# Spreading a unit's decay logarithms by one product, and adding the state sum earlier, in a chunked mLSTM with two expert layers behind it

## The chip, the cores and the metric

The kernel runs on one core of a Trainium2 chip. The metric is the device time of the whole program in microseconds. A core has a matrix engine (PE, with its weight loads shown apart as PEld), a vector engine (DVE), a scalar engine (ACT), a general engine (POOL), and a sync engine (SP) that here only issues DMAs. Each engine runs its own instructions strictly in the order in which they were issued to it. Whatever is needed from another engine is waited for by semaphores.

## The reference, cut to what matters

Three stages follow one another: a gated linear attention (mLSTM) with a running stabiliser, an expert layer in which tokens are assigned greedily under a capacity, and a dense layer with an ELU.

```python
for t in range(S):                         # B=4, H=8, S=768, D=40
    m_new  = np.maximum(f_gate[:, :, t] + m, i_gate[:, :, t])
    f_stab = np.exp(f_gate[:, :, t] + m - m_new)
    i_stab = np.exp(i_gate[:, :, t] - m_new)
    C = f_stab[..] * C + i_stab[..] * (v k^T)
    n = f_stab[..] * n + i_stab[..] * k
    y[:, :, t] = sigmoid(o) * (C q) / np.maximum(np.abs(n q), 1.0)
# x = y as (3072, 320)
logits = x @ w_gate                        # 8 experts, 384 tokens each, greedy by logit
out[mask] = np.maximum(x[mask] @ w1[e], 0.0) @ w2[e]
h = out @ w_in;  g = elu(h);  result = g @ w_out
```

## The kernel before

The attention is done in chunks of 64 tokens: twelve chunks, and for each chunk two units of 2 batches by 8 heads, so 24 units. Unit u is chunk u // 2. The two batches of a unit lie on partitions 0 to 63 and 64 to 127. `Attention.run` is a pipeline over units written out by hand: iteration u works on unit u and prepares u + 1 (called v) and u + 2 (called w). Nothing reorders it; the order of the calls is the order on each engine.

What the names are, by the lines of the profile:

- **Logarithms.** `maximum` (L233) scans the stabiliser m. `logs` (L242 to L248) makes the decay logarithm ac and the input logarithm gi on 32 rows (batch and head). `split` (L257 to L264) writes each as three bfloat16 parts, fp and pb, on 96 rows; each part is copied by ACT and subtracted by DVE (L260, L261).
- **Decay weights.** `decay(w)` (L310 to L316) builds in one bank pF the logarithm of the 64 x 64 decay matrix of all 8 heads: a mask (L310), eight products of 64 columns, one for each head, whose stationary operand `sel` picks the head's rows of fp (L312), and a product for the inputs' side (L314). ACT takes the exponential (W, L316). `decays` (L323 to L334) makes the decays Dt and De over whole chunks.
- **Scores and values.** `scores(w)` (L301) and `values(u)` (L376) are interleaved on PE. `weigh(v)` (L355) multiplies scores by W into P, which `values(v)` needs in the next iteration.
- **State.** `recall(v)` (L390) is q times the state C of the chunk before, and is interleaved with `state(u)` (L403), the unit's own contribution pC. `seed(v)` (L366) writes the decayed recall into the output bank pO, on which `values(v)` then accumulates. `fade(v)` (POOL: L343 kt, L345) prepares the decayed keys and the decayed old state. `add_state(u)` (L414; L416 in the first chunk) adds pC to it. That sum is what `recall` of unit u + 2 reads, in the next iteration.
- **Output.** `gates(u)` (L423 to L428 on DVE, L429 on POOL) makes x; `turn` (L445) transposes it in the next iteration, and `logits` (L459) follows.
- **Fill.** From iteration 2 on, pieces of the later stages' weights are converted between the attention's own steps by `fl(i)`. The weights arrive as 8 bytes for a number; a piece takes ACT cg (L918), ACT cF (L925), DVE cF (L931), DVE cF (L934), ACT wih (L999) and POOL wil (L1001), or similar lines. `early` (L656 to L676) sorts finished logits.

The order on DVE within iteration u, from L502 on, is weigh(v), gates(u), seed(v), then the fill pieces, and add_state(u) behind them. `logs` and `split` over the ten later chunks (640 columns) stand at the start and in iterations 0 to 2.

After the attention come the first routing round and then the two layers, whose order is set by a planner with fixed costs; there the instructions of each engine stay as they are.

Of the kernel before, what the change touches and what calls it, by code (L numbers as in the profile page):

```python
# [8 lines left out]
F32 = mybir.dt.float32  # L9
F32R = mybir.dt.float32r  # L10
BF = mybir.dt.bfloat16
# [108 lines left out]
class Attention:  # L120
# [4 lines left out]
    def __init__(self, nc, tc, consts, qk, vk, ig, fg, wg, xd, L, ident):  # L125
# [50 lines left out]
        V.tensor_tensor(pair, i3[:, :16], i3[:, 16:], op=ALU.add)  # L176
        self.sel = one.tile([96, 16, 2, 64], BF, name="sel")
        V.tensor_copy(self.sel, i3.rearrange("p (r m) -> p m r", r=2)[:, :, :, None].to_broadcast([96, 16, 2, 64]))
        self.one_m = one.tile([96, 16, 64], BF, name="one_m")
# [10 lines left out]
        self.wr = one.tile([96, 2, 64], BF, name="wr")  # L190
        A.activation(self.wr, self.half[:, :, None].to_broadcast([96, 2, 64]), AF.Copy)
        self.i3 = i3
        self.Dt = one.tile([128, NS, 16], F32, name="Dt")
# [42 lines left out]
    def logs(self, n0, n1):  # L236

        gi, gf, m, keep, ac = self.g
        V = self.nc.vector
        a, b = n0 * 64, n1 * 64  # L240
        t = slice(a, b)
        V.tensor_tensor(gf[:, t], gf[:, t], m[:, t], op=ALU.add)  # L242
        V.tensor_tensor(gf[:, t], gf[:, t], m[:, a + 1:b + 1], op=ALU.subtract)
        if n0 == 0:
            V.memset(gf[:, 0:1], 0.0)
        V.tensor_tensor_scan(ac[:, t], keep[:, t], gf[:, t], 0.0, op0=ALU.mult, op1=ALU.add)
        V.tensor_tensor(gi[:, t], gi[:, t], m[:, a + 1:b + 1], op=ALU.subtract)
        V.tensor_tensor(gi[:, t], gi[:, t], ac[:, t], op=ALU.subtract)  # L248

    def split(self, n0, n1):  # L250

        gi, gf, m, keep, ac = self.g
        A, V = self.nc.scalar, self.nc.vector
        t = slice(n0 * 64, n1 * 64)
        for k in range(3):
            p, q = self.fp[k * 32:k * 32 + 32, t], self.pb[k * 32:k * 32 + 32, t]
            A.activation(p, ac[:, t], AF.Copy)  # L257
            A.activation(q, gi[:, t], AF.Copy)
            if k < 2:
                V.tensor_tensor(ac[:, t], ac[:, t], p, op=ALU.subtract)  # L260
                V.tensor_tensor(gi[:, t], gi[:, t], q, op=ALU.subtract)  # L261
                yield
        for r in range(2):
            A.activation(self.fb[:, n0:n1, r], self.pb[:, t].rearrange("p (n t) -> p n t", t=64), AF.Copy,  # L264
                         scale=self.half[:, r:r + 1])

    def load_qk(self, u):
# [37 lines left out]
    def decay(self, u):  # L305
# [4 lines left out]
        PE.matmul(p, self.idb, self.low, start=True, stop=False)  # L310
        for h in range(8):
            PE.matmul(p[:, h], self.sel[:, bp * 8 + h].rearrange("p r t -> p (r t)"), self.fp[:, n * 64:n * 64 + 64],  # L312
                      start=False, stop=False)
        PE.matmul(p, self.fb[:, n].rearrange("p r t -> p (r t)"), self.one_m[:, bp * 8:bp * 8 + 8], start=False, stop=True)  # L314
        self.W[u] = self.two.tile([128, 8, 64], F32, name="W", bufs=3)
        A.activation(self.W[u], p, AF.Exp)  # L316

    def decays(self, n0, n1):

        A, PE = self.nc.scalar, self.nc.tensor  # L320
        k = n1 - n0
        x = self.two.tile([96, 16, 10], BF, name="fx", bufs=1)[:, :, :k]
        self.nc.vector.tensor_tensor(x, self.one_m[:, :, :k], self.fp[:, None, n0 * 64 + 63:n1 * 64:64].to_broadcast([96, 16, k]),  # L323
# [7 lines left out]
        e = p[:, 256:256 + k * 16]  # L331
        PE.matmul(e, self.wr.rearrange("p r t -> p (r t)"), x.rearrange("p m n -> p (m n)") if k == 10 else x[:, :, 0], start=True, stop=True)
        A.activation(self.De[:, :, n0:n1], e.rearrange("p (m n) -> p m n", n=k), AF.Exp)
# [141 lines left out]
    def run(self, hook, fill, pull):  # L475
        later = self.split(2, NS)
        self.zeros(0)
        for u in range(NU):
# [4 lines left out]
            self.both(self.values(u), self.scores(w))  # L483
            if u == 0:
                self.decays(1, 2)
            if u < 3:
                next(later, None)
            if v < NU:
# [1112 lines left out]
```

## Time and profile before

| | |
|---|---|
| three runs | 763.69, 769.18 and 766.97 us, median 766.97 |
| the profiled execution | 769.29 us, of it 767.5 us span |
| attention, 24 units | about 0 to 154 us |
| routing round and first gathers | about 154 to 194 us |
| the two layers | about 194 to 767 us |

The page gives each engine's busy time and 40 slices of the span. Busy shares are means over stages with different limits, so each stage is read by itself. In the layers PE is busy nearly all the time. In the attention no engine is, and the rows on waits and on single units say what ends each step.

### The profile page before, as it was taken

The page shows a single profiled execution, that of the slowest core. Times are in us where ns is not written, and L with a number is a line of the kernel's source. Part 1 is how long each engine was busy: PE and PEld are TensorE (multiplying, and loading weights), DVE is VectorE, ACT ScalarE, POOL GpSimd, SP SyncE. Part 2 cuts the span into 40 slices and gives each one's busy share as a digit, 9 for nine tenths or more (in the row PEclk, how much of TensorE's full clock was granted, in tenths as well). Part 3 has the DMA queues.
Part 4 walks back from the last instruction along what each step waited for, and adds up shares of the span by engine and source line. Part 5 has one row for each costly group of instructions (what it writes and reads, how often), then busy time and mean ns, then how long its engine had stood idle before and what let it go on. Part 6 is the DMA issues. An engine that isn't in the chain of part 4 may idle for free.

```text
span 767.5 us, 17906 instructions
## 1 busy us (share of the span) xinstructions
PE 702.1 (91%) x7228; PEld 640.0 (83%) x7232; DVE 536.9 (70%) x1610; ACT 377.3 (49%) x804; POOL 180.1 (23%) x242
## 2 busy tenths in 40 slices
PE   6787888834999999999999999999999999999994
PEld 4555666622989998999999999999999999999994
DVE  8674787677878878875796698669768834841551
ACT  5553544423555735751673376256527734742542
POOL 5473643226111310401221120112022220001001
PEclk9999999955999999999999999999999999999998
DMA  9686878125200500500220220022013321100000
GB/s 310 201 256 197 241 206 249 39 80 166 95 0 6 173 26 1 177 1 27 83 95 27 72 82 25 26 83 95 1 44 106 108 82 34 36 0 26 1 1 26
DMA packets 22435, 67.29 MB, mean 88 GB/s; under 512 B 3536, under 2 KB 7632, under 8 KB 22352
## 3 DMA queue, kind: packets, MB, share of 16 engines
q1 hardware_dynamic: 14240, 35.12, 15.2%
q0 software_dynamic: 8064, 30.94, 12.3%
q8 instruction: 56, 0.92, 0.5%
q14 instruction: 27, 0.22, 0.1%
q10 hardware_dynamic: 48, 0.10, 0.0%
HBM read 58.28 MB, written 7.86 MB: 86 GB/s over the span
## 4 chain that ended last, share of the span: by engine, by line
PE 69%; DVE 12%; issue 11%; ACT 4%; DMA 2%; POOL 1%; POOLq 0%; ACTq 0%; DVEq 0%
PE ph L1176 31%; PE acc L1315 6%; PE acc L1319 6%; PE acc L1316 6%; PE acc L1283 3%; PE acc L1285 2%; PE acc L1284 2%; PE pR L390 2%; PE pO L376 1%; PE acc L1270 1%; PE pX L445 1%; PE acc L1272 1%; PE ph L1129 1%; DVE C L414 1%; PE pr L773 1%
## 5 line engine op out<-in xcount | busy, mean ns | idle before, releaser
L1229 DVE SCALAR_TENSOR_TENSOR e<-e,ph 128x384 f32<-128x384 f32 x128 | 70.4, 550 | 51.6 <-ACT e L1226 50.9
L1225 ACT ACTIVATE e<-ph 128x384 f32<-128x384 f32 x128 | 62.3, 487 | 80.7 <-PE ph L1176 75.8
L1176 PE MATMUL ph<-yh,wih 128*128 128x384 f32 x256 | 89.5, 349 | 0.6 <-DVE xl L1137 0.3
L1193 ACT ACTIVATE gh<-ph 128x384 fp32r<-128x384 f32 x64 | 31.5, 491 | 115.1 <-PE ph L1176 90.4
L1176 PE MATMUL ph<-yh,wil 128*128 128x384 f32 x256 | 86.6, 338 | 0.0
L1325 POOL DMA_INDIRECT out_dram<-ot,idx x24 | 24.0, 998 | 218.8 <-ACT ot L1046 215.9
L1053 DVE TENSOR_TENSOR gl<-e,gh 128x384 fp32r<-128x384 f32 x128 | 71.0, 561 | 1.8 <-ACT gh L1046 0.3
L1226 ACT ACTIVATE e<-e 128x384 f32<-128x384 f32 x128 | 67.3, 526 | 4.0
L1315 PE MATMUL acc<-woh,gh 128*128 128x320 f32 x216 | 68.3, 316 | 0.0
L1200 DVE SCALAR_TENSOR_TENSOR gl<-ph,gh 128x384 fp32r<-128x384 f32 x64 | 35.2, 552 | 45.8 <-ACT gh L1193 45.7
L1319 PE MATMUL acc<-woh,gl 128*128 128x320 f32 x216 | 66.8, 309 | 0.4 <-DVE gl L1053 0.4
L1316 PE MATMUL acc<-wol,gh 128*128 128x320 f32 x216 | 66.7, 309 | 0.0
L1176 PE MATMUL ph<-yl,wih 128*128 128x384 f32 x256 | 66.5, 341 | 0.0
L1046 ACT ACTIVATE gh<-e 128x384 fp32r<-128x384 f32 x96 | 49.0, 514 | 11.4 <-DVE e L1229 11.1
L1319 PE MATMUL acc<-woa,gl 128*128 128x320 f32 x168 | 52.4, 312 | 0.8 <-DVE gl L1053 0.8
L1315 PE MATMUL acc<-woa,gh 128*128 128x320 f32 x168 | 53.1, 316 | 0.0
L1176 PEld LDWEIGHTS ph<-yh,wih 128*128 128x128 f32 x256 | 48.2, 188 | 4.7 <-ACT yh L1288 4.1
L1316 PE MATMUL acc<-wob,gh 128*128 128x320 f32 x168 | 51.9, 309 | 0.0
L1176 PEld LDWEIGHTS ph<-yh,wil 128*128 128x128 f32 x256 | 48.1, 188 | 0.0
L1176 PEld LDWEIGHTS ph<-yl,wih 128*128 128x128 f32 x256 | 46.2, 188 | 0.0
L1176 PE MATMUL ph<-xh,w1h 128*128 128x384 f32 x128 | 44.9, 351 | 0.0
L1176 PE MATMUL ph<-yh,wis 128*128 128x384 f32 x128 | 44.8, 350 | 0.0
(282 smaller groups left out, 1992.0 us busy)
## 6 DMA issues: line engine op xcount, KB each, us to landing
vk<-in_vk_dram SPq DMA_DIRECT2D x24, 484.0 KB, 5.6
qk<-in_qk_dram SPq DMA_DIRECT2D x20, 320.0 KB, 5.6
cx<-in_win_dram SPq DMA_DIRECT2D x8, 512.0 KB, 5.6
xd<-x SPq DMA_DIRECT2D x48, 80.0 KB, 3.8
wx<-in_wout_dram SPq DMA_DIRECT2D x9, 320.0 KB, 3.0
cx<-in_wout_dram SPq DMA_DIRECT2D x5, 448.0 KB, 5.2
qk<-in_qk_dram SPq DMA_DIRECT2D x4, 512.0 KB, 6.4
cx<-in_win_dram SPq DMA_DIRECT2D x4, 256.0 KB, 5.5
```

The costliest lines, as they stand in the source:

```text
L1046: self.nc.scalar.activation(out, x, AF.Copy)
L1053: self.nc.vector.tensor_tensor(out, x, y, op=ALU.subtract)
L1176: PE.matmul(p, w, x, start=k == 0, stop=k == 7)
L1193: nc.scalar.activation(h, p, AF.Relu)
L1200: nc.vector.scalar_tensor_tensor(l, p, 0.0, h, op0=ALU.max, op1=ALU.subtract)
L1225: nc.scalar.activation(e, p, AF.Relu, scale=-1.0)
L1226: nc.scalar.activation(e, e, AF.Exp, scale=-1.0)
L1229: nc.vector.scalar_tensor_tensor(e, e, -1.0, p, op0=ALU.add, op1=ALU.max)
L1315: PE.matmul(p, h[:, c], wh, start=f == 0, stop=False)
L1316: PE.matmul(p, h[:, c], wl, start=False, stop=False)
L1319: PE.matmul(p, l[:, c], wh, start=False, stop=f == 15)
L1325: s = nc.gpsimd.indirect_dma_start(out=self.out, out_offset=bass.IndirectOffsetOnAxis(ap=idx[:, t:t + 1], axis=0), in_=o, in_offset=None)
```

## The change

There are three parts. First, the eight products of 64 columns in `decay` become one of 512. For that `spread(n)` writes, once for a chunk, fe = heads x fp (96 rows, 512 columns, with each head's own rows only); chunk 0 on DVE, the other eleven on POOL, in odd iterations between fade(v) and gates(u). The stationary operand ws is one of two small constants. `sel` goes; `head`, `side`, `heads` and `ws` come. Second, the logarithms are made in three parts (chunks 0 to 1, 2 to 3 and 4 to 11) instead of two; the last part (512 columns) is computed in iterations 2 to 5. Third, `add_state(u)` moves from behind the fill pieces to right behind `seed(v)`.

```diff
-        self.sel = one.tile([96, 16, 2, 64], BF, name="sel")
-        V.tensor_copy(self.sel, i3.rearrange(...).to_broadcast([96, 16, 2, 64]))
+        V.tensor_tensor(head, pair[:, :8], pair[:, 8:], op=ALU.add)
+        V.tensor_reduce(side, pair.rearrange("p (b h) -> p b h", b=2), AX, ALU.max)
+        A.activation(self.head, head[:, :, None].to_broadcast([96, 8, 64]), AF.Copy)
...
+        for b in range(2):
+            A.activation(self.ws[b], self.wr, AF.Copy, scale=side[:, b:b + 1])
...
-        self.logs(0, 2)
-        for _ in self.split(0, 2):
+        for _ in self.decay_logs(0, 2):
             pass
+        self.spread(0, V)
...
         V.memset(self.pC, 0.0)
-        V.memset(self.pX, 0.0)
         self.decay(1)
         self.both(self.scores(1))
+        self.decays(1, 2)
         self.weigh(0)
+        V.memset(self.pX, 0.0)
         self.fade(0)
-        self.logs(2, NS)
+        self.spread(1, G)
+        for _ in self.logs(2, 4):
+            pass
...
-        for h in range(8):
-            PE.matmul(p[:, h], self.sel[:, bp * 8 + h]..., self.fp[:, n * 64:n * 64 + 64], ...)
+        PE.matmul(p, self.ws[bp].rearrange("p r t -> p (r t)"), self.fe[n], start=False, stop=False)
...
+    def spread(self, n, engine):
+        self.fe[n] = self.two.tile([96, 8, 64], BF, name="fe")
+        engine.tensor_tensor(self.fe[n], self.head, self.fp[:, None, n * 64:n * 64 + 64].to_broadcast([96, 8, 64]), op=ALU.mult)
...
     def run(self, hook, fill, pull):
-        later = self.split(2, NS)
+        later = {0: self.split(2, 4), 2: self.decay_logs(4, NS)}
+        when = [(0, 2), (0, 1), (2, 2), (2, 2), (2, 1), (2, 1)]
...
             if u == 2:
-                self.decays(2, NS)
+                self.decays(2, 4)
+            if u == 6:
+                self.decays(4, NS)
             if v < NU:
                 self.weigh(v)
+            if u < 6:
+                which, parts = when[u]
+                for _ in range(parts):
+                    next(later[which], None)
...
             if v < NU:
                 self.fade(v)
+            if u % 2 and u // 2 + 2 < NS:
+                self.spread(u // 2 + 2, self.nc.gpsimd)
             self.gates(u)
             if v < NU:
                 self.seed(v)
+            self.add_state(u)
             fl(1)
             fl(5)
             fl(2)
             if u > 0:
                 self.logits(u - 1)
-            self.add_state(u)
             fl(3)
```

The first place is DVE in iteration 7, from the seed of unit 8 to the seed of unit 9. C is the state sum, A a step of the early sorting, cF the conversion of a weight piece, P the weighed scores, rd and x the gates. Before:

```order
L366 TENSOR_TENSOR pO<-pR,Dt 128x8x41
L931 SCALAR_TENSOR_TENSOR cF<-cx,cF 128x512
L676 TENSOR_TENSOR A<-w_291,a_1147 128x32
L934 SCALAR_TENSOR_TENSOR cF<-cg,cF 128x512
L414 TENSOR_TENSOR C_170<-C_170,pC 128x8x41
L355 TENSOR_TENSOR P<-pS,W 128x512
L423 TENSOR_SCALAR rd<-pO 128x8
```

In the changed kernel, where the same lines are L388, L958, L703, L961, L436, L377 and L445:

```order
L388 TENSOR_TENSOR pO<-pR,Dt 128x8x41
L436 TENSOR_TENSOR C_178<-C_178,pC 128x8x41
L958 SCALAR_TENSOR_TENSOR cF<-cx,cF 128x512
L703 TENSOR_TENSOR A<-w_297,a_1126 128x32
L961 SCALAR_TENSOR_TENSOR cF<-cg,cF 128x512
L377 TENSOR_TENSOR P<-pS,W 128x512
L445 TENSOR_SCALAR rd<-pO 128x8
```

The state sum now stands ahead of the conversion; P still stands behind it.

The second place is DVE in iteration 3 of the changed kernel, from the state sum of unit 2 to the gates of unit 3. Before, the same stretch was:

```order
L414 TENSOR_TENSOR C_168<-C_168,pC 128x8x41
L355 TENSOR_TENSOR P<-pS,W 128x512
L423 TENSOR_SCALAR rd<-pO 128x8
L424 SCALAR_TENSOR_TENSOR rd<-pO,rd 128x8
L425 RECIPROCAL rd<-rd 128x8
L428 SCALAR_TENSOR_TENSOR x<-sg,pO 128x320
L366 TENSOR_TENSOR pO<-pR,Dt 128x8x41
```

Now:

```order
L436 TENSOR_TENSOR C_176<-C_176,pC 128x8x41
L958 SCALAR_TENSOR_TENSOR cF<-cx,cF 128x512
L961 SCALAR_TENSOR_TENSOR cF<-cg,cF 128x512
L377 TENSOR_TENSOR P<-pS,W 128x512
L260 TENSOR_TENSOR gi<-gi,m 32x512
L261 TENSOR_TENSOR gi<-gi,ac 32x512
L273 TENSOR_TENSOR ac<-ac,fp 32x512
L274 TENSOR_TENSOR gi<-gi,pb 32x512
L445 TENSOR_SCALAR rd<-pO 128x8
L446 SCALAR_TENSOR_TENSOR rd<-pO,rd 128x8
L447 RECIPROCAL rd<-rd 128x8
L450 SCALAR_TENSOR_TENSOR x<-sg,pO 128x320
```

Four logarithm steps of 512 columns now stand between P and the gates. In iteration 2 three others (L253, L254 and L258) stand at the same place, and in iteration 4 two.

The third place is POOL in iteration 7 (kt, the faded state and the gates' last product; wil belongs to the fill). Before:

```order
L343 TENSOR_TENSOR kt_178<-vk,W 128x8x40
L345 TENSOR_TENSOR C_168<-C_167,De 128x8x41
L429 TENSOR_TENSOR x<-x,rd 128x320
L1001 TENSOR_TENSOR wil<-cF,wih 128x512
L343 TENSOR_TENSOR kt_179<-vk,W 128x8x40
```

Now:

```order
L365 TENSOR_TENSOR kt_186<-vk,W 128x8x40
L367 TENSOR_TENSOR C_176<-C_175,De 128x8x41
L338 TENSOR_TENSOR fe<-heads,fp 96x512
L451 TENSOR_TENSOR x<-x,rd 128x320
L1028 TENSOR_TENSOR wil<-cF,wih 128x512
L365 TENSOR_TENSOR kt_187<-vk,W 128x8x40
```

The product fe stands ahead of the gates' product, in every second iteration.

## Rows read from the trace of the kernel before

**Rows 1.** The page, parts 1 and 2: PE's busy time; DMA share by slices.

```profile
PE 702.1 (91%) x7228; PEld 640.0 (83%) x7232; DVE 536.9 (70%) x1610; ACT 377.3 (49%) x804; POOL 180.1 (23%) x242
...
DMA  9686878125200500500220220022013321100000
```

**Rows 2.** Busy times by stretch: the attention without its start and end.

```profile
core 0: us, PE busy (x) PEld busy (x) DVE busy (x) ACT busy (x) POOL busy (x), PEclk, DMA share, GB/s
...
25.00:150.00 125.00, 101.68 (x3052) 74.77 (x3046) 86.14 (x219) 59.90 (x125) 58.97 (x68) 0.97 0.71 209
```

**Rows 3.** Waits, 25 to 150 us: us in total, times, longest.

```profile
DVE cF L931 <- ACT cF L925: 23.6, 10, 3.7
...
PE pR L390 <- DVE C L414: 12.1, 13, 2.1
...
PE pR L390 <- issue: 2.6, 2, 1.7
```

**Rows 4.** DVE in time, iterations 7 and 8: start, duration, what; idle before.

```profile
60.12 0.51 DVE L366 TENSOR_TENSOR pO<-pR,Dt 128x328 f32<-128x328 f32 x1 [1.47 <-PE pR L390]
63.51 0.69 DVE L931 SCALAR_TENSOR_TENSOR cF<-cx,cF 128x512 int32<-128x512 int32 x1 [2.89 <-ACT cF L925]
...
64.24 0.69 DVE L934 SCALAR_TENSOR_TENSOR cF<-cg,cF 128x512 int32<-128x512 int32 x1
64.85 0.49 DVE L414 TENSOR_TENSOR C<-C,pC 128x328 f32<-128x328 f32 x1
...
66.37 0.45 DVE L428 SCALAR_TENSOR_TENSOR x<-sg,pO 128x320 f32<-128x320 f32 x1
67.30 0.51 DVE L366 TENSOR_TENSOR pO<-pR,Dt 128x328 f32<-128x328 f32 x1 [0.48 <-PE pC L403]
```

**Rows 5.** PE, the first recall of unit 9.

```profile
65.39 0.27 PE L390 MATMUL pR<-C,qk 64*64 64x64 f32 x2 [1.76 <-DVE C L414]
```

**Rows 6.** DVE, the start of the program.

```profile
2.68 1.27 DVE L178 COPY sel<-i 96x2048 bf16<-96x2048 bf16 x1
...
5.80 0.28 DVE L248 TENSOR_TENSOR gi<-gi,ac 32x128 f32<-32x128 f32 x1
...
10.02 0.66 DVE L355 TENSOR_TENSOR P<-pS,W 128x512 f32<-128x512 f32 x1
10.61 0.80 DVE L242 TENSOR_TENSOR gf<-gf,m 32x640 f32<-32x640 f32 x1
...
14.52 1.24 DVE L248 TENSOR_TENSOR gi<-gi,ac 32x640 f32<-32x640 f32 x1
...
18.56 0.67 DVE L355 TENSOR_TENSOR P<-pS,W 128x512 f32<-128x512 f32 x1
...
22.78 0.67 DVE L355 TENSOR_TENSOR P<-pS,W 128x512 f32<-128x512 f32 x1
```

**Rows 7.** DVE, P of units 4 and 23.

```profile
34.84 0.68 DVE L355 TENSOR_TENSOR P<-pS,W 128x512 f32<-128x512 f32 x1
...
147.94 0.68 DVE L355 TENSOR_TENSOR P<-pS,W 128x512 f32<-128x512 f32 x1
```

**Rows 8.** PE, the last two of the three steps of one decay.

```profile
48.47 0.40 PE L312 MATMUL pF<-fp,sel 96*128 96x64 bf16 x8
48.70 0.38 PE L314 MATMUL pF<-one_m,fb 96*128 96x512 bf16 x1
```

**Rows 9.** A DVE and a POOL instruction at one time, from both engines' order of time.

```profile
82.38 1.19 DVE L666 TENSOR_TENSOR e<-e,w 128x32 f32<-128x32 f32 x1
...
82.23 1.29 POOL L1001 TENSOR_TENSOR wil<-cF,wih 128x512 fp32r<-128x512 f32 x1
```

**Rows 10.** Durations in ns, minimum, median and maximum, by line.

```profile
L429 POOL TENSOR_TENSOR x<-x,rd x24: 717/722/1200, 20.2 to 154.7; 128x320 f32<-128x320 f32 x24
...
L355 DVE TENSOR_TENSOR P<-pS,W x24: 661/681/692, 10.0 to 147.9; 128x512 f32<-128x512 f32 x24
...
L934 DVE SCALAR_TENSOR_TENSOR cF<-cg,cF x15: 607/681/1022, 33.8 to 143.2; 128x512 int32<-128x512 int32 x10, 128x448 int32<-128x448 int32 x5
```

More of the change, by code (lines that the diff above doesn't have):

```diff
@@ L176, in __init__ @@
         V.tensor_tensor(pair, i3[:, :16], i3[:, 16:], op=ALU.add)
-        self.sel = one.tile([96, 16, 2, 64], BF, name="sel")
-        V.tensor_copy(self.sel, i3.rearrange("p (r m) -> p m r", r=2)[:, :, :, None].to_broadcast([96, 16, 2, 64]))
+        head = one.tile([96, 8], BF, name="head")
+        V.tensor_tensor(head, pair[:, :8], pair[:, 8:], op=ALU.add)
+        side = one.tile([96, 2], F32, name="side")
+        V.tensor_reduce(side, pair.rearrange("p (b h) -> p b h", b=2), AX, ALU.max)
+        self.head = one.tile([96, 8, 64], BF, name="heads")
+        A.activation(self.head, head[:, :, None].to_broadcast([96, 8, 64]), AF.Copy)
         self.one_m = one.tile([96, 16, 64], BF, name="one_m")
@@ L191, in __init__ @@
         A.activation(self.wr, self.half[:, :, None].to_broadcast([96, 2, 64]), AF.Copy)
+        self.ws = [one.tile([96, 2, 64], BF, name=f"ws{b}") for b in range(2)]
+        for b in range(2):
+            A.activation(self.ws[b], self.wr, AF.Copy, scale=side[:, b:b + 1])
         self.i3 = i3
@@ L209, in __init__ @@
         self.maximum(0, 128)
-        self.logs(0, 2)
-        for _ in self.split(0, 2):
-            pass
+        for _ in self.decay_logs(0, 2):
+            pass
+        self.fe = {}
+        self.spread(0, V)
         self.opens(0)
@@ L245, in logs @@
             V.memset(gf[:, 0:1], 0.0)
+        yield
         V.tensor_tensor_scan(ac[:, t], keep[:, t], gf[:, t], 0.0, op0=ALU.mult, op1=ALU.add)
+        yield
         V.tensor_tensor(gi[:, t], gi[:, t], m[:, a + 1:b + 1], op=ALU.subtract)
@@ L265, in split, with decay_logs @@
                          scale=self.half[:, r:r + 1])
+    def decay_logs(self, n0, n1):
+        yield from self.logs(n0, n1)
+        yield
+        yield from self.split(n0, n1)
     def load_qk(self, u):
@@ L310, in decay @@
         PE.matmul(p, self.idb, self.low, start=True, stop=False)
-        for h in range(8):
-            PE.matmul(p[:, h], self.sel[:, bp * 8 + h].rearrange("p r t -> p (r t)"), self.fp[:, n * 64:n * 64 + 64],
-                      start=False, stop=False)
+        PE.matmul(p, self.ws[bp].rearrange("p r t -> p (r t)"), self.fe[n], start=False, stop=False)
         PE.matmul(p, self.fb[:, n].rearrange("p r t -> p (r t)"), self.one_m[:, bp * 8:bp * 8 + 8], start=False, stop=True)
@@ L321, in decays @@
         k = n1 - n0
-        x = self.two.tile([96, 16, 10], BF, name="fx", bufs=1)[:, :, :k]
+        x = self.two.tile([96, 16, k], BF, name=f"fx{k}", bufs=1)
         self.nc.vector.tensor_tensor(x, self.one_m[:, :, :k], self.fp[:, None, n0 * 64 + 63:n1 * 64:64].to_broadcast([96, 16, k]),
@@ L331, in decays @@
         e = p[:, 256:256 + k * 16]
-        PE.matmul(e, self.wr.rearrange("p r t -> p (r t)"), x.rearrange("p m n -> p (m n)") if k == 10 else x[:, :, 0], start=True, stop=True)
+        PE.matmul(e, self.wr.rearrange("p r t -> p (r t)"), x.rearrange("p m n -> p (m n)"), start=True, stop=True)
         A.activation(self.De[:, :, n0:n1], e.rearrange("p (m n) -> p m n", n=k), AF.Exp)
@@ L483, in run @@
             self.both(self.values(u), self.scores(w))
[L484 to L487, printed above, removed]
             if v < NU:
```

## The prediction

> **What bounds the kernel now.** I read the page first. PE is busy 91% of the span, but the slices of DMA show that loading is heavy in the first eight or so and light afterwards [rows 1]: the attention is one stage, the layers another. The change touches only the first 150 us, so the page's 91% says nothing about it. The busy times by stretch come next. From 25 to 150 us PE is busy 101.68 of 125 us, DVE 86.14, POOL 58.97 [rows 2]. No engine is full, so waits decide. The iterations from P of unit 4 (34.84) to P of unit 23 (147.94) take 113.1 us [rows 7], 5.95 us for each of 19.
>
> The view of waits tells which waits stand there. PE waits 12.1 us, 13 times, to begin `recall` until the state sum on DVE is done, and 2.6 us for nothing that the profile shows; DVE waits 23.6 us for the weight pieces from ACT [rows 3]. The unit view joins them. DVE finished the seed at 60.63, idled until ACT gave the piece at 63.51, did L931 and L934, and only then the state sum at 64.85 [rows 4]. PE stood 1.76 us and began the recall at 65.39 [rows 5]. The sum's own inputs were there long before: it stood idle behind a piece of weight conversion, by order alone.
>
> **The change part by part.**
>
> *The state sum moves up.* It follows the seed, so it could run at 60.6 instead of 64.85. What PE gains is the 1.76 us of [rows 5] here and 12.1 us in all [rows 3], if nothing else is late. What is late next: P still stands behind the piece. Without the sum in front of it (0.40 us from start to start [rows 4]), P begins 0.4 earlier, the gates end 0.4 earlier (66.4 in place of 66.82), and the next seed, which waited for PE until 67.30, may run at 66.4, 0.9 earlier and not 1.76. `values` needs that seed. So between a half and all of each wait comes back: in this unit PE's own work (transposes, decay, logits) still lies between recall and values, which covers the difference; where the early sorting or logarithms add DVE work, it does not. I take half of 12.1, 6.0 us, with ends 0 and 12.1.
>
> *The logarithms in three parts.* Before, DVE does five steps of 640 columns between the first and second P, from 10.61 to 15.7, and then waits for and does the first of the parts; the second P comes 8.5 us after the first and the third at 22.78 [rows 6]. Now five steps of 128 columns stand there, at 0.28 us each, about 1.5 us [rows 6]. `sel` goes (1.19 us from its start to the next step [rows 6]), but three more ACT copies and fe of chunk 0 on DVE, about 0.6 us by P's 0.66 on 512 columns [rows 6], come into the same chain; I count these as even. The second P then comes some 5 us earlier, and the third too. But the work is moved, not removed: the 512-column part is four fifths of the 640-column one. Of five steps that took 5.1 us, 4.1 remain, and four part subtractions come to 2.6, by four fifths of L242's 0.80 each [rows 6]. They now stand in iterations 2, 3 and 4 between P and the gates, on the way to the seed, which values waits for. In iteration 3 the part copies on ACT also stand behind W. DVE was idle there for a few microseconds, but ahead of the weight pieces, not ahead of the gates. So I let the 5 us of the start be given back by iteration 5, with 0.5 us left: -0.5, ends -4 and +1.5.
>
> *One product of 512 columns in place of eight of 64.* The eight start at 48.47 and the next step at 48.70: 0.23 us for all eight. The 512-column product behind them has 0.38 us against 0.40 for the group [rows 8]. The same columns at the same pace, so PE gains nothing; 24 x 0.0. Its weight loads lie under the product before. Fourteen instructions fewer per unit may move the unexplained PE stalls of [rows 3] by 2 us either way.
>
> *Spread on POOL.* Eleven products of 96 x 512 in bfloat16 with two inputs. No row has this form. From the 320-column product, 0.72 us [rows 10], and the 512-column one, 1.29 us [rows 9], I take 1.2; ends 0.7 and 1.3. POOL is busy less than half of the time [rows 2], and the product that needs fe comes an iteration later, so POOL's own time costs nothing. But the rows show a coupling: at 82.38 a DVE product of 32 columns took 1.19 us and ended with POOL's, which had run since 82.23 for 1.29 [rows 9]. L934, which reads two tiles of SBUF, takes 607 to 1022 ns; P, which reads one of its inputs from PSUM, 661 to 692, never more [rows 10]. So fe can hold the conversions and the logarithms, and not the seed, the sum, the gates or P themselves. Eleven times 1.2 is 13.2 us if each fe holds one such step on the path in full. Since it meets only these steps, I take a quarter, +3.3; ends 0 and 13.2.
>
> The rule to weigh here is the Trainium skill's, SBUF — State Buffer, section "SBUF: two separate sides": VectorE and GpSimd share one port pair, and whoever comes first holds it for its whole instruction while the other waits. Rows 9 and 10 agree with it. It speaks against this change, and what it would make of the time is the third rival.
>
> *Sum.* -6.0 - 0.5 + 0.0 + 3.3 = -3.2 us. The profiled execution took 769.29 us, so 766.1; it stands 2.3 above the median of the runs shown, 766.97. In terms of the median that is 763.8. The stages behind the attention begin when the last logits are there and keep their order, so what the attention gains is passed on whole: **764 us**.
>
> **Rivals.** All are given against the median.
>
> First, everything pays. All 12.1 us come back, the start keeps 1 us and fe meets nothing on the path: -13.1, **754 us**. For it: the units' PE work is shorter than 5.95 us without the waits (101.68 busy in 125 [rows 2] is 4.8 per iteration). Against: with PE at 4.8, the way through ACT's piece, L931, L934, P, gates and seed is hardly shorter.
>
> Second, nothing pays. DMA is busy six to nine tenths in the first eight slices [rows 1], and 0.71 in [rows 2]; an attention of shorter iterations needs its loads sooner and gets them at the same pace, or PE's unexplained stalls grow with them. The 6 us become waits on loads: **767 us**. For it: the slices with 9. Against: no wait of [rows 3] is on a load.
>
> Third, slower: the coupling of POOL and DVE. fe is ahead of the gates' product on POOL and meets the conversions. If two thirds of the eleven hold a step on the path, that is 8.8 us; conversions that are held also hold P, so of the 12.1 us only 3 come back. -3.0 - 0.5 + 8.8 = +5.3, **772 us**. It decides from the point at which three of the eleven are held in full, 3.6 us against 3.5. For it: [rows 9, 10]. Against: in a unit like that of [rows 4] the piece waits for ACT, not for POOL.
>
> That the one product does not do the work of eight is not a case that I can see; that it costs PE the same is part of the forecast.
>
> **How the numbers follow.** Forecast 0.50, everything pays 0.20, nothing pays 0.17, slower 0.13. A measurement of this kernel can tell about 1%, 7.7 us, from no change: under 759.3 is faster, over 774.6 slower. Faster: 0.16 from the first rival and 0.04 from the good end of the forecast, 0.20. Slower: a third of the third rival, 0.04, and 0.01 for what I have not seen, 0.05. Same 0.75. The forecast's own range is 759 to 768. The whole range takes in the better half of the first rival's times only from 755 on, and the third up to 770: low **755**, high **770**, with about 0.12 and 0.08 left out.
>
> **What would show it.** The wait of `recall` on the state sum should fall from 12.1 us to under 2. The wait of `values` on the seed should rise to several microseconds, above all in iterations 2 to 4, where P of unit 5 should come no earlier than one or two microseconds before its old time although the second P came some 5 earlier. The 512-column product should take 0.38 us. fe on POOL should take about 1.2 us, and L931, L934 and the logarithm steps beside it should reach 1.0 us or more. If the second P is not earlier, the start is misread; if fe takes 2 us or more, or the seed itself is lengthened, the slower rival holds; if P of unit 5 keeps 4 us of the start, the first.

## The result and the profile after

The changed kernel takes 778.66 us (median of 4 runs, 776.10 to 779.88) where the kernel before took 767.04 beside it: ratio 1.0139, 95% interval 1.0101 to 1.0178. The change is 8 to 14 us slower. The prediction was 764 us with a range of 755 to 770, so it was wrong in sign and in size. The profiled execution took 779.71 us, 777.9 of it span.

The page of the changed kernel, parts 1 and 2: busy times, and TensorE's granted clock by slices.

```profile
PE 707.5 (91%) x7054; PEld 639.8 (82%) x7065; DVE 545.3 (70%) x1622; ACT 379.2 (49%) x817; POOL 190.7 (25%) x253
...
PEclk9779979985899999999999999999999999999998
```

PE is busy 5.4 us longer than in [rows 1] although it has 174 products fewer. Six of the first eleven slices hold digits of 5 to 8 in the row of the clock; before there were two, both in the routing round. The layers have none up to the last slice. The busy times by stretch say the same for the attention's middle:

```profile
core 0: us, PE busy (x) PEld busy (x) DVE busy (x) ACT busy (x) POOL busy (x), PEclk, DMA share, GB/s
25.00:150.00 125.00, 96.90 (x2581) 68.57 (x2591) 90.06 (x201) 57.80 (x122) 67.62 (x74) 0.86 0.70 203
```

Against [rows 2], PE does less in the same 125 us (2581 products in place of 3052, of which the eight products made one account for some 130), at a clock of 0.86 in place of 0.97. Neither DVE nor POOL is full. So waits decide again, and there are others now. Waits of PE and of DVE, 25 to 150 us (total, times, longest):

```profile
PE pO L398 <- DVE pO L388: 10.9, 5, 3.3
PE pR L351 <- DVE pO L388: 5.9, 2, 3.3
PE pX L467 <- issue: 4.7, 1, 4.7
...
DVE cF L958 <- ACT cF L952: 14.1, 7, 2.9
DVE fx L345 <- ACT fp L270: 5.1, 2, 2.9
DVE ac L273 <- ACT fp L270: 4.5, 2, 2.5
```

The wait of `recall` for the state's sum, 12.1 us in [rows 3], is gone. In its place PE waits 16.8 us for the seed (L388): in the values (L398) and in the decays (L351), up to 3.3 us at a time. DVE waits less for weight pieces (14.1 against 23.6), and now also 9.6 us for the part copies of the logarithms on ACT (L270): 4.5 us in the subtractions of `split` (L273), and 5.1 us in fx (L345), the first step of `decays`, which stands ahead of P in iterations 2 and 6.

Where the time went is seen from P. P of units 1, 2, 5, 8 and 23 in the changed kernel (DVE in order of time):

```profile
13.21 0.67 DVE L377 TENSOR_TENSOR P<-pS,W 128x512 f32<-128x512 f32 x1
20.34 0.68 DVE L377 TENSOR_TENSOR P<-pS,W 128x512 f32<-128x512 f32 x1
...
47.09 0.69 DVE L377 TENSOR_TENSOR P<-pS,W 128x512 f32<-128x512 f32 x1
...
69.74 0.68 DVE L377 TENSOR_TENSOR P<-pS,W 128x512 f32<-128x512 f32 x1
...
161.33 0.68 DVE L377 TENSOR_TENSOR P<-pS,W 128x512 f32<-128x512 f32 x1
```

Unit 1 is 5.3 us earlier than in [rows 6], unit 2 2.4. Before, units 5 and 8 had their P at 42.36 and 57.06. So unit 5 is 4.7 us late and unit 8 12.7; unit 23 is 13.4 late [rows 7]. From unit 2 to unit 8 some 15 us are lost. The start's lead is gone by unit 3, whose P, at 25.45, is on its old time of 25.42, before any logarithm step of 512 columns has run: in iteration 0 the part copies on ACT stand behind W, and the gates begin 5.87 us after P. From unit 3 to unit 8 12.7 us are lost. Behind unit 8 the lag moves by some 4 us either way and ends near where it was.

One iteration shows how. DVE in iteration 3, from P of unit 4 to the state's sum:

```profile
35.76 0.68 DVE L377 TENSOR_TENSOR P<-pS,W 128x512 f32<-128x512 f32 x1
36.36 0.67 DVE L260 TENSOR_TENSOR gi<-gi,m 32x512 f32<-32x512 f32 x1
37.07 1.67 DVE L261 TENSOR_TENSOR gi<-gi,ac 32x512 f32<-32x512 f32 x1
40.79 0.90 DVE L273 TENSOR_TENSOR ac<-ac,fp 32x512 f32<-32x512 f32 x1 [2.06 <-ACT fp L270]
41.62 0.67 DVE L274 TENSOR_TENSOR gi<-gi,pb 32x512 f32<-32x512 f32 x1
42.23 0.15 DVE L445 TENSOR_SCALAR rd<-pO 128x8 f32<-128x8 f32 x1
...
43.09 0.50 DVE L388 TENSOR_TENSOR pO<-pR,Dt 128x328 f32<-128x328 f32 x1
43.50 0.49 DVE L436 TENSOR_TENSOR C<-C,pC 128x328 f32<-128x328 f32 x1
```

The gates (L445) begin 6.47 us after P. In the kernel before they began 0.6 us after it. Of the 6.47, four logarithm steps take 3.9, and 2.06 is a wait for ACT, whose copy L270 stands behind W of unit 5, and that behind PE's decay. PE, which needs the seed for the values of unit 4, stood meanwhile:

```profile
43.65 0.27 PE L398 MATMUL pO<-vk,P 64*64 64x64 f32 x2 [3.21 <-DVE pO L388]
```

In iterations 2, 3 and 4 the distance from P to the gates is 5.35, 6.47 and 4.53 us, against 0.62, 0.60 and 0.60 before: 14.5 us more. What the values wait for is the seed. It came 6.19, 7.33 and 5.40 us after P, against 3.90, 1.47 and 1.48: 12.1 us more. In iteration 2 it was late before too, since it waited for PE (DVE in the kernel before):

```profile
29.32 0.51 DVE L366 TENSOR_TENSOR pO<-pR,Dt 128x328 f32<-128x328 f32 x1 [2.33 <-PE pC L403]
```

The 12.1 us are about the size of what is lost between units 3 and 8. In iteration 4 the wait for ACT is longer than the steps, and in iteration 6, where the decays of the last eight chunks now stand, DVE waits for the last part copy ahead of P of unit 7 (DVE in the changed kernel):

```profile
50.23 0.68 DVE L273 TENSOR_TENSOR ac<-ac,fp 32x512 f32<-32x512 f32 x1 [2.45 <-ACT fp L270]
...
61.32 0.40 DVE L345 TENSOR_TENSOR fx<-one_m,fp 96x128 bf16<-96x128 bf16 x1 [2.89 <-ACT fp L270]
61.63 0.69 DVE L377 TENSOR_TENSOR P<-pS,W 128x512 f32<-128x512 f32 x1
```

P of unit 6 is 8.6 us late, P of unit 7 11.8. By this trace the new place of the decays takes part in the loss; no run moves it alone.

Some of these steps are also longer than their work. A step of 512 columns begins in iteration 2 beside POOL, from the orders of DVE and POOL in time:

```profile
26.05 2.42 DVE L253 TENSOR_TENSOR gf<-gf,m 32x512 f32<-32x512 f32 x1
```
```profile
25.39 1.17 POOL L338 TENSOR_TENSOR fe<-heads,fp 96x512 bf16<-96x512 bf16 x1 [3.17 <-ACT fp L270]
26.52 0.71 POOL L451 TENSOR_TENSOR x<-x,rd 128x320 f32<-128x320 f32 x1
27.20 0.73 POOL L365 TENSOR_TENSOR kt<-vk,W 128x320 f32<-128x320 f32 x1
27.90 1.19 POOL L367 TENSOR_TENSOR C<-C,De 128x328 f32<-128x328 f32 x1
```

The step took 2.42 us where one of its kind without POOL beside it took 0.67 (L274 in iteration 3 above). It began during the first of four POOL products that ran without a gap, and ended 0.54 us after the third. The fourth took 1.19 us, where it took 0.75 in iteration 3, which fits DVE having its turn there and POOL being held in its place. The Trainium skill, SBUF — State Buffer, section "SBUF: two separate sides", says that the engine which comes first holds the shared ports for its whole instruction. The trace agrees that DVE is held, and goes further: DVE was passed over by two more POOL instructions behind the one that it met, so the price is not bounded by that one. How many can pass it no run here shows.

The parts that the prediction priced by rows are as said: the product of 512 columns and fe (PE in time; durations in ns, minimum, median and maximum):

```profile
77.82 0.38 PE L330 MATMUL pF<-fe,ws 96*128 96x512 bf16 x1
78.04 0.38 PE L331 MATMUL pF<-one_m,fb 96*128 96x512 bf16 x1
```
```profile
L338 POOL TENSOR_TENSOR fe<-heads,fp x11: 1147/1158/1612, 10.7 to 144.2; 96x512 bf16<-96x512 bf16 x11
L338 DVE TENSOR_TENSOR fe<-heads,fp x1: 421/421/421, 7.8 to 7.8; 96x512 bf16<-96x512 bf16 x1
```

### The profile page after: what moved, and what is told of

The parts are those of the page before. It is cut to its first block, busy times and chain, and to the rows that moved or that the text cites. A ratio compares the mean times of both kernels' runs of the same rounds, so it can differ in the third digit from the quotient of the medians.

```text
span 777.9 us, 17606 instructions
## 1 busy us (share of the span) xinstructions
PE 707.5 (91%) x7054; PEld 639.8 (82%) x7065; DVE 545.3 (70%) x1622; ACT 379.2 (49%) x817; POOL 190.7 (25%) x253
## 3 DMA queue, kind: packets, MB, share of 16 engines
q0 software_dynamic: 8064, 30.94, 12.1%
## 4 chain that ended last, share of the span: by engine, by line
PE 71%; issue 11%; DVE 9%; ACT 4%; DMA 1%; POOL 1%; POOLq 0%; ACTq 0%; DVEq 0%
PE ph L1203 31%; PE acc L1342 6%; PE acc L1346 6%; PE acc L1343 6%; PE acc L1310 3%; PE acc L1312 2%; PE acc L1311 2%; PE pR L412 2%; PE pO L398 2%; PE acc L1297 1%; PE pX L467 1%; PE acc L1299 1%; PE ph L1156 1%; PE pr L800 1%; DVE cF L958 1%
## 5 line engine op out<-in xcount | busy, mean ns | idle before, releaser
L1073 ACT ACTIVATE gh<-e 128x384 fp32r<-128x384 f32 x96 | 49.0, 514 | 11.4 <-DVE e L1256 11.1
L1084 POOL DMA_INDIRECT stg<-in_w1a_dram,wi x16 | 15.7, 982 | 122.5 <-DVE wi L838 118.2
```

What stands on the lines that cost most here:

```text
L1073: self.nc.scalar.activation(out, x, AF.Copy)
```

## The experiments

All ratios are to the kernel before, run beside it; its medians in these groups lie between 766.2 and 768.9 us, so kernels of different groups are compared by their ratios. A trace shows one execution, which can lie some us from the median. L numbers are those of the changed kernel unless said otherwise.

### The three parts alone

**The state's sum alone.** The kernel before with

```diff
             if v < NU:
                 self.seed(v)
+            self.add_state(u)
...
                 self.logits(u - 1)
-            self.add_state(u)
```

> The kernel before, with the state's sum moved behind the seed and nothing else. Theory A (late log pieces and the clock): the sum's move is a gain, as the prediction had it, 3 to 12 us, so 755 to 764; PE's wait of 12.1 us for the sum falls to under 2, and half-speed stretches in the first 155 us stay at about three. Theory B (POOL's spread holds DVE) says the same. Theory C (the move itself harms, since PE reaches the values earlier and waits for the seed longer, and the clock then falls): 770 or more, with waits of values on the seed of over 5 us.

Measured: 767.78 us, 0.9984 (0.9960 to 1.0008), 1.2 us less and hardly to be told from nothing. The wait for the sum is gone, yet PE's waits from 17 us to the last x sum to 22.1 us in place of 25.3. The seed's went from 1.8 to 5.1 and those without a named cause from 5.5 to 9.4. Two of its rows of PE's waits, 17 to 150 us (in this kernel L376 is the values, L366 the seed):

```profile
PE pO L376 <- DVE pO L366: 5.1, 5, 2.3
...
PE pO L376 <- DMA vk<-in_vk_dram: 1.5, 1, 1.5
```

P of unit 13 came 5.0 us earlier than before, P of unit 15 only 0.7. Theory C, harm by the move, falls; theory A's 3 to 12 us are met only at their lower end by the interval (3.1 us), and not by the median.

**The logarithms alone.** The changed kernel with `sel` and the eight products back, and `add_state` at its old place:

```diff
+        for h in range(8):
+            PE.matmul(p[:, h], self.sel[:, bp * 8 + h]...
-        PE.matmul(p, self.ws[bp]..., self.fe[n], ...)
...
-            if u % 2 and u // 2 + 2 < NS:
-                self.spread(u // 2 + 2, self.nc.gpsimd)
...
-            self.add_state(u)          # behind seed(v)
+            self.add_state(u)          # behind logits(u - 1)
```

> The kernel before, with the logarithms in three parts and nothing else: the eight products of 64 columns stay, and the state's sum stays where it was. Theory A: this part carries the loss. P of unit 1 comes about 5 us earlier than before, P of unit 8 about 10 us later; PE waits 3 us each for the seed in iterations 2 to 4, TensorE's granted clock is at its lower level for 25 us or more of the first 160; 775 to 785. Theory B: no loss without the spread, 762 to 768. Theory C: the same as theory B.

Measured: 776.22 us, 1.0104 (1.0076 to 1.0132), 8.0 us more. P of unit 1 is 5.6 us early, of unit 8 8.8 us late. The distance from P to the gates is 3.17, 5.10 and 4.16 us in iterations 2 to 4. DVE waits for ACT ahead of P of unit 7 here too (fx, 2.50 us). This part carries most of the loss, as theory A had it. But the granted clock is at its lower level for only 14 us in the first 150, not the 25 and more that A expected. Also here, without any fe, POOL holds a step (L250 is this kernel's line for L260, L1013 the weight pieces' product), DVE and then POOL in time:

```profile
34.65 1.67 DVE L250 TENSOR_TENSOR gi<-gi,m 32x512 f32<-32x512 f32 x1
```
```profile
34.47 1.31 POOL L1013 TENSOR_TENSOR wil<-cF,wih 128x512 fp32r<-128x512 f32 x1 [6.13 <-ACT wih L1011]
```

**The spread alone.** The kernel before with ws, heads, fe and the one product:

```diff
-        for h in range(8):
-            PE.matmul(p[:, h], self.sel[:, bp * 8 + h]...
+        PE.matmul(p, self.ws[bp]..., self.fe[n], start=False, stop=False)
...
+            if u == 2:
+                self.spread(2, self.nc.vector)
...
+            if u > 1 and u % 2 and u // 2 + 2 < NS:
+                self.spread(u // 2 + 2, self.nc.gpsimd)
             self.gates(u)
```

> The kernel before, with the one product of 512 columns and its factor fe (chunk 0 and, since the logarithms stay in two parts, chunk 2 on DVE, the others on POOL) and nothing else. Theory A: fe of 1.2 us holds a DVE step now and then, 765 to 770, and half-speed stretches stay at about three. Theory B: fe on POOL is what lengthens DVE's steps and so carries the loss, 774 to 782. Theory C: 767.

Measured: 772.71 us, 1.0053 (1.0028 to 1.0078), 4.1 us more: between theory A and theory B. The three parts alone make 8.0 + 4.1 - 1.2 = 10.9 us; the whole change makes 10.7. The sum agrees, though each part is known to about 2 us only; the next run leaves open whether they simply add up.

**The logarithms and the sum, without the spread.** The kernel with the logarithms alone, and `add_state` behind the seed.

> The changed kernel without the spread: the logarithms in three parts and the state's sum behind the seed, with the eight products and no fe at all. By adding up the parts alone (logarithms 1.0104, sum 0.9984): 1.0088, 774. If the sum's move, with steps between P and the gates, only turns the recall's wait into a wait of values on the seed: 774 to 777. If POOL's fe is what makes the steps cost (theory H): 766 to 770.

Measured: 778.12 us, 1.0133 (1.0086 to 1.0180). Its interval takes in the sum of the two parts (1.0088), and also a sum's move that brings nothing here (1.0104). By the ratios it takes as long as the whole change (1.0139): the 4.1 us of the spread do not show on top of these two parts, though the intervals leave room for them. Theory H falls: without any fe the loss stays. PE's wait for the seed in iteration 3 is 4.5 us, in a trace of an execution of 770.81 us, the fastest of the six by nearly 5.

### The granted clock

**Two fills.** The changed kernel, with products of zeros where PE stood:

```diff
+KEEP = {2: 12, 3: 16, 4: 16, 6: 12}
...
+            if u in (2, 6):            # ahead of the decays; for 3 and 4 behind the logits
+                for _ in range(KEEP[u]):
+                    self.nc.tensor.matmul(self.pX[:, :384], self.wz[:, :128], self.wz[:, :384], ...)
```

> The changed kernel, with products of zeros into an unused part of a PSUM tile at the four places where PE stood for about 3 us (12 of 384 columns ahead of the decays of iterations 2 and 6, 16 behind the logits of iterations 3 and 4); nothing reads them. Theory A with the clock as amplifier: PE's waits stay, but the granted clock stays at 2.4 GHz between 28 and 70, the steps there shorten, and 3 to 8 us of the loss of 11.6 come back: 771 to 776. If the waits alone make the loss (the clock beside it costs nothing, because DVE sets the pace there): 778 to 780. Theory B: 778 to 780 as well.

Measured: 778.58 us, 1.0146 (1.0113 to 1.0179), as if the clock cost nothing; but its own products waited in iteration 4. The second one writes into pF, with `KEEP = {2: 10, 3: 14, 4: 14, 6: 10}` and 512 columns.

> The changed kernel with products of zeros that nothing reads at the four places where PE stood for about 3 us, now into the PSUM tile of the decays, which is free there (10 of 512 columns ahead of the decays of iterations 2 and 6, 14 behind the logits of iterations 3 and 4). In the first such kernel the products of iteration 4 themselves waited 3.25 us for a copy on ACT. If the granted clock costs time there: it stays at 2.4 GHz from 28 to 70, and 770 to 776. If DVE sets the pace there whatever the clock: 777 to 780.

Measured: 777.01 us, 1.0113 (1.0065 to 1.0161). Busy times of the changed kernel and of the second fill, 28 to 70 us:

```profile
28.00:70.00 42.00, 28.23 (x648) 20.43 (x653) 28.89 (x65) 19.47 (x41) 19.48 (x20) 0.78 0.59 173
```
```profile
28.00:70.00 42.00, 35.91 (x771) 21.75 (x776) 28.62 (x69) 19.12 (x41) 21.01 (x22) 0.96 0.66 195
```

The clock is back at 0.96 (in the first fill too), DVE does the same work, and P of unit 8 is still 9.0 us late, in the first fill 11.1, in place of 12.7. The low clock, at 1.2 in place of 2.4 GHz in parts of these 42 us, followed PE's stands: from 28 to 32 PE was busy 0.93 us, and from 32 to 36 the clock was 0.50. It comes with the loss; that it adds to it is not shown. The second time lies at the edge between the two forecasts. The ratios tell no gain, but each is known to 0.4 or 0.5% only, and in both traces P of unit 23 is 8.6 us late in place of 13.4. So most of the loss is there at the full clock too, where DVE's order sets the pace; whether the clock adds some us stays open.

### The place of the steps, and who computes fe

**Behind the seed, the logarithms alone.**

```diff
-            if u < 6:
-                which, parts = when[u]
-                for _ in range(parts):
-                    next(later[which], None)
...
             if v < NU:
                 self.seed(v)
+            if u < 6:
+                which, parts = when[u]
+                for _ in range(parts):
+                    next(later[which], None)
```

> The kernel with the logarithms in three parts alone (776.2, 1.0104 of before), with the steps of iterations 0 to 5 moved from between P and the gates to behind the seed. Theory A' (the place: between P and the gates they delay the seed, for which the values wait): most of the 8 us come back, 766 to 771, PE's waits of 3 us for the seed in iterations 3 and 4 go, and P of unit 8 comes no later than 2 us after its time before. Theory D (the amount: DVE and ACT have no room for these steps in iterations 2 to 5, wherever they stand): 774 to 778, P of unit 8 still 7 us or more late.

Measured: 773.83 us, 1.0133 (1.0082 to 1.0185): nothing comes back, and P of unit 8 is 8.0 us late. The gates follow P after 0.6 us in iterations 2 to 4, as before, but the state's sum now stands behind the steps, and `recall` waits for it (PE's waits, 17 to 150 us; L399 is recall, L423 the sum in this kernel):

```profile
PE pR L399 <- DVE C L423: 13.9, 11, 2.8
```

Two of these waits, 2.5 and 2.8 us, stand in iterations 4 and 5, where the kernel with the steps ahead of the gates waited 3.1 and 3.3 us for the seed. Theory A' falls in this form: the steps only moved from ahead of one thing that PE needs to ahead of another. Theory D, the amount, stands after this run; the next ones decide.

**Behind the state's sum, in the changed kernel,** with fe behind them and still on POOL: the same lines, moved behind `self.add_state(u)`.

> The changed kernel with the logarithms' steps of iterations 0 to 5, and fe behind them, moved behind the state's sum; fe stays on POOL. The kernel with this and fe on DVE took 0.9984 of before, 12 us less than the change. Theory G (the place is what counts, and it needs the state's sum ahead of the steps, since behind them the recall waits for the sum): 765 to 770. Theory H (fe on POOL is what counts): 774 to 779. Both a part: 770 to 774.

Measured: 769.95 us, 1.0020 (0.9988 to 1.0051). Nine of the 10.7 us are gone, and P of unit 8 is 3.8 us late in place of 12.7. The same steps cost little here, so theory D falls.

**fe on DVE, steps where the change put them:**

```diff
-        self.spread(1, G)
+        self.spread(1, V)
...
-                self.spread(u // 2 + 2, self.nc.gpsimd)      # ahead of gates(u)
+                self.spread(u // 2 + 2, self.nc.vector)      # behind add_state(u)
```

> The changed kernel with every fe on DVE, behind the state's sum, and the logarithms' steps where the change put them, between P and the gates. Theory G: the loss stays, 774 to 779, with PE's waits of 3 us for the seed in iterations 3 and 4. Theory H: 765 to 770. Both a part: 770 to 774.

Measured: 774.74 us, 1.0077 (1.0044 to 1.0109), at the edge between theory G and a part for both.

**Both.**

> The changed kernel with both: the logarithms' steps behind the state's sum and every fe on DVE behind them. Theory A' with B: the start's 5 us are kept and the costs of steps and fe go, so 760 to 766, under both kernels. Theory A' with a limit by the loads (the loads come one for each P and find DMA busy 0.8 to 0.9): 765 to 769. Theory D: 774 or more.

Measured: 765.92 us, 0.9984 (0.9950 to 1.0018), where the first two forecasts meet. The four kernels make a table:

| | fe on POOL | fe on DVE |
|---|---|---|
| steps between P and the gates | 1.0139 | 1.0077 |
| steps behind the state's sum | 1.0020 | 0.9984 |

The place is worth 0.9 to 1.2%, the engine of fe 0.4 to 0.6%. Theory G is shown for the larger part: in each column the intervals lie apart. The part copies on ACT move with the steps, and fe on POOL goes behind the gates' product with them, so the place is that of the whole group and not of DVE's steps alone. For the engine the intervals of each pair still overlap, and the kernel without any fe (1.0133) is no faster than the one with fe on POOL (1.0139); a cost of the engine is not shown.

**fe on DVE with the spread alone,** the same edit there:

> The kernel with the spread alone (772.7, 1.0053 of before), with every fe computed on DVE, from iteration 3 on behind the seed, and none on POOL. On DVE the first fe took 0.42 us, on POOL 1.15. Theory B (POOL's fe holds DVE's steps): DVE pays 11 times 0.4 to 0.7, mostly in its idle time, and 2 us or more come back: 768 to 771. Theory E (the cost is at the start: fe of chunk 0 and the copies on ACT ahead of the first P, fe of chunk 2 between the conversions): no change, 772 to 774.

Measured: 770.86 us, 1.0063 (1.0031 to 1.0095), against 1.0053 with POOL: no gain. So in that kernel POOL's fe isn't the cause of the 4 us. By the time theory E fits, and P of unit 1 is 1.2 to 1.4 us late in both. By the traces it does not: P of unit 3 is 3.8 to 3.9 us late, but P of unit 10 is 0.9 us early with fe on POOL and 1.1 late with fe on DVE. In both, the lag grows by some 3.5 us between the P of units 13 and 14. There, with fe on POOL (PE in time; the stretch; DVE in time, where L379 is the seed, L403 the recall and L458 the transposes):

```profile
86.69 0.30 PE L458 MATMUL pX<-ident,x 128*64 128x128 f32 x1 [1.62 <-issue]
```
```profile
88.00:92.00 4.00, 4.00 (x114) 3.09 (x115) 2.42 (x8) 1.14 (x3) 2.78 (x4) 0.57 1.02 257
```
```profile
93.40 0.51 DVE L379 TENSOR_TENSOR pO<-pR,Dt 128x328 f32<-128x328 f32 x1 [1.84 <-PE pR L403]
```

PE stood 1.62 us for nothing that the trace names, ran at a granted clock of 0.57 where before it had 1.00 in this stretch, and the seed waited for its recall. Whether the spread brings this about is not shown; the cause of the 4 us stays open.

### Where the gain of the state's sum goes

**Earlier loads.** The kernel with the sum's move alone, and

```diff
-            if 0 < u < NU - 4:
-                self.load_vk(u + 4)
+            if u < NU - 5:
+                self.load_vk(u + 5)
```

> The kernel with the state's sum moved alone (767.8, 0.9984 of before; its lead of 5 us at unit 13 was lost by unit 15, where values waited 1.5 us for a load of vk), with every load of vk from unit 5 on issued one iteration earlier. If the lateness of single loads takes the lead: 762 to 765, and P of unit 15 comes 4 us or more before its time in the kernel before. If it is the pace of all loads, or ACT's and DVE's conversion steps in iterations 13 and 14, that takes it: 767 to 769.

Measured: 766.97 us, 1.0018 (0.9992 to 1.0044). No wait for a load of vk is left in its trace, and nothing is gained; but PE's waits without a named cause rose from 9.4 to 14.6 us, so this speaks against the lateness of single loads and does not settle it.

**Fewer loads,** before and with the sum's move:

```diff
             if u + 5 < NU:
-                self.load_qk(u + 5)
+                if u < 4:
+                    self.load_qk(u + 5)
+                else:
+                    self.QK[u + 5] = self.QKb[(u + 5) % 4]
```

> The kernel before without the loads of qk from unit 9 on (15 loads of 320 KB; units from 9 on compute with the queries and keys of earlier units), to see whether loads set the attention's pace. If the pace of loads, or stalls of PE under them, counts: 760 to 764. If not: 766 to 769.

> The kernel with the state's sum moved alone, also without the loads of qk from unit 9 on. If the gain of the sum's move was lost to loads (PE's waits that the trace names no cause for rose from 5.5 to 9.4 us, and one of 1.5 for a load came): 4 to 7 us less than the same kernel without the move, 755 to 760, and the unnamed waits fall. If it was lost to the next wait on DVE and ACT (the seed): 0 to 2 us less than that kernel.

Measured: 764.56 us, 0.9963 (0.9937 to 0.9990), and 761.12 us, 0.9922 (0.9890 to 0.9953). With fewer loads the move is worth 3.4 us in place of 1.2, between the two forecasts (4 to 7 and 0 to 2), and P of unit 15 keeps 3.0 us of lead over the kernel without it where it kept 0.7. It speaks for the loads taking some of the gain, but the two intervals overlap. PE's waits without a named cause fell from 5.5 to 2.2 us without the move, and hardly with it (8.2 us against 9.4). What these waits are stays open.

**POOL's order.** Here `fade(v)` is issued ahead of the fill:

```diff
-            fl(0)
             if v < NU:
                 self.fade(v)
+            fl(0)
```

> The kernel with late steps and fe on DVE, with POOL's kt and faded state issued ahead of the weight pieces' product. In that kernel PE stood 3.2 us at 30.4 until kt, which lay on POOL behind that product, itself waiting for ACT. If POOL's order costs: 760 to 764, under the kernel before. If the stall only moves: 765 to 767.

> The kernel with the state's sum moved alone and the same order on POOL. If POOL's order held units there too: 762 to 765. If not: 766 to 769.

Measured: 762.90 us, 0.9934 (0.9899 to 0.9970), and 764.81 us, 0.9971 (0.9947 to 0.9996). The first beats both kernels: 4.6 us under the kernel before, and by the two ratios 2% under the change. Against the same kernel without this order (0.9984) the intervals overlap. Its iteration 3 on DVE:

```profile
32.82 0.69 DVE L377 TENSOR_TENSOR P<-pS,W 128x512 f32<-128x512 f32 x1
33.42 0.16 DVE L445 TENSOR_SCALAR rd<-pO 128x8 f32<-128x8 f32 x1
...
34.30 0.50 DVE L388 TENSOR_TENSOR pO<-pR,Dt 128x328 f32<-128x328 f32 x1
34.71 0.49 DVE L436 TENSOR_TENSOR C<-C,pC 128x328 f32<-128x328 f32 x1
35.11 1.03 DVE L260 TENSOR_TENSOR gi<-gi,m 32x512 f32<-32x512 f32 x1
...
37.91 1.22 DVE L273 TENSOR_TENSOR ac<-ac,fp 32x512 f32<-32x512 f32 x1 [1.05 <-ACT fp L270]
```

The seed starts 1.48 us after P in place of 7.33. The steps are still held by POOL (1.03, 1.22) and still wait for ACT, but PE no longer waits behind them. Its P of unit 8 is at 58.65, 1.6 us after the kernel before: the work is paid for, and the start's lead of 5.3 us covers most of it. That kt behind the weight pieces was the reason of the 3.2 us stall is not shown: in the new order a stall of 2.97 us stands at the same place, ahead of the transposes of iteration 3, at 32.2.

## Why the prediction was wrong

**The step that failed is the logarithms in three parts**: "I let the 5 us of the start be given back by iteration 5, with 0.5 us left: -0.5, ends -4 and +1.5". Alone they cost 8.0 us (5.8 to 10.1 by the interval), outside both ends. The start was read rightly as far as P of unit 1, which came 5.3 us earlier in the changed kernel; the P after it, which was to keep the lead too, came 2.4 us earlier, and the next one on its old time. The prediction also said that the steps stand between P and the gates, on the way to the seed, that DVE's idle time lies elsewhere, and that the part copies stand behind W on ACT. Then it priced them by their durations, moved work against moved work, 4.1 and 2.6 us. The runs showed in its place that steps ahead of the seed cost the whole time that they hold it, waits included: 12.1 us by the trace. What was missing:

- Two of the pairs wait for ACT, 2.06 us in iteration 3 and 2.45 in iteration 4. That the copies stand behind W had been named, and the wait was not priced. The decays, whose fx waits 2.25 and 2.89 us for the same copies ahead of P in iterations 2 and 6, had not been named at all.
- Steps with two tiles of SBUF as inputs were held by POOL (2.42 and 1.67 us for 0.67). The coupling had been charged to fe alone, though kt, the faded state, x and the weight pieces' product run on POOL whatever fe does; the 1.67 us are beside the last of these.
- Of the 14.5 us from P to the gates, 12.1 reach the seed, and PE, which runs in order, stands until it is there (3.2 to 3.3 us each for the seeds of iterations 2 to 4). At the start the same work had cost P of unit 1 some 5 us.

**The state's sum**: -6.0 forecast, -1.2 measured (-3.1 to +0.6). The mechanism was right: `recall`'s wait fell from 12.1 us to none, and the values' wait for the seed rose. The share was too large. Half of a wait was counted as a gain, but its place was taken by the seed (3.3 us more), by PE's waits without a named cause (3.9 us more), and by a load (0.5 us more). Rival two, "nothing pays", was right for this part, and the runs with fewer loads support its reason in part only. Two readings there were loose: of the first eight slices of DMA in [rows 1] the eighth has one tenth, and the view of [rows 3] also has a wait of 1.0 us on a load of vk, below the lines shown.

**The one product**: right, 0.38 us for 0.38; no run has it without fe.

**fe and the spread**: +3.3 forecast, +4.1 measured alone, and 1.16 us for each fe against an estimate of 1.2. That the size came out is luck as far as the runs show: in the kernel with the spread alone, fe on DVE brings nothing back, so fe's hold on DVE, which the term stood for, is not what cost the 4 us; beside the other two parts no cost of the spread shows, and fe on DVE there brings 0.4 to 0.6%, 3 to 5 us, of which the intervals leave open whether it is anything.

**The third rival** (772 us, POOL and DVE) had the right side and a piece of the right mechanism. But it held the conversions to be what is hit. Some were (L958 took 1.25 and 1.79 us at 44.73 and 53.44, for 0.69), though not beside fe but beside the faded state and the weight pieces' product; the logarithm steps were too, and most of the loss needs no fe at all. No rival reached the measured time.

**The signs it named** came as it said: `recall`'s wait went, the seed's rose above all in iterations 2 to 4, the product took 0.38 us and fe 1.2. P of unit 5 was to come no earlier than a microsecond or two before its old time; it came 4.7 us after it, which meets the words and not the half microsecond of lead that the sum kept.

TensorE's clock is not in the prediction at all. By the fills most of the loss is there without the low clock; that none of it is the clock's they do not show.

## What to carry to other kernels

Price a step that moves between two links of a chain by the time from link to link, with the waits for other engines inside it, not by its duration: here 3.9 us of steps made 6.5 us of distance. Before moving work into an idle stretch, look at which side of the next needed result the stretch lies on, and move that result ahead: behind both seed and sum the steps cost about what the start had gained by them, and ahead of either they were dear. And a wait that disappears is a gain only up to the next wait on the same engine: here 12.1 us of wait gave 1.2, by the interval at most 3.1.

## What the runs showed of the hardware

- A DVE step that meets POOL can be held through POOL instructions that follow without a gap (two more, 2.42 us for 0.67), not only through the one that it meets. The hold goes the other way too: the POOL product behind these took 1.19 us for 0.75.
- The product of 96 x 512 in bfloat16, with one operand repeated over heads, took 0.42 us on DVE and 1.16 us on POOL, 2.8 times as long. Where it ran on DVE beside POOL's product of the gates (the kernel with the spread alone), it took 0.75.
- PE stood up to 4.72 us (at 93.9 us in the changed kernel, ahead of the transposes) for nothing that the trace names. Such stands came in every kernel, 2.2 to 14.6 us in all, most where the loads were issued earlier.
- 42 us in which the mean granted clock was 0.78, brought back to 0.96 by products of zeros, gave no gain that these runs can tell (1.0146 and 1.0113 against 1.0139, each known to 0.4 or 0.5%). PE was waiting for DVE in parts of them.
